# A hand-written order of the opening: the spare maximum on GpSimd earlier, the last copies of x ahead of the transposing DMAs, tiles 12 to 15 split sooner

## The chip, the cores and the metric

One core of a Trainium2 chip runs the kernel. The metric is device time in microseconds (us) of one execution. TensorE (PE) does the matrix products, VectorE (DVE), ScalarE (ACT) and GpSimd (POOL) the elementwise work, SyncE (SP) issues most DMAs, and POOL issues the DMAs that add to memory while they write.

## The reference

A layer norm over 576 features of 2048 rows, and the sum of three terms: x itself, the real part of a two-dimensional DFT of the normed x, and a two-layer MLP of the normed x with 4608 hidden features.

```python
xn = _layernorm(x, axis=-1)
return x + _A_ref(xn, A_dft_seq_re, A_dft_seq_im, A_dft_hid_re, A_dft_hid_im) + _B_ref(xn, B_w1, B_w2)
# _A_ref: a = xn @ re.T, b = xn @ im.T, y = Cr @ a - Ci @ b
# _B_ref: h = max(xn @ w1, 0), y = h @ w2
```

## The kernel before, in words

Every f32 operand is split into two f16 parts, `hi` and `lo`, and a product is made of three f16 products. x is cut into 16 tiles of 128 rows; four tiles are a group (g = 0 to 3). The hidden features are cut into nine blocks. For each block and group the kernel makes the first layer (line 380, eight banks of PSUM in two pools of four), splits the result, and makes the second layer (line 643) as seven products of a Strassen-like scheme over half matrices. Behind the MLP comes the DFT with the same scheme. This text is only about the opening, the first 90 us or so, in which block 0 is worked off for groups 0 to 2.

What happens to a tile t in the opening: `counts` and `moments` take mean and variance on DVE, `stats` does the rest of the layer norm in small steps (one step serves a whole group for tiles 4 to 15), `normal` writes the normed tile in f32, `high_x` its f16 part, `low_x` the difference in two pieces (part 1 has 512 columns, part 0 has 64), `again` copies 128 columns once more. Then the tile is transposed: tiles 0 to 3 by PE, tiles 4 to 15 by a DMA that SP issues (`transposes_dma`, line 336). The four staging places for this lie in one buffer, `dbuf`; tile t uses place t % 4. The split of block 1's w1 (`split_w1`, lines 232 on ACT and 235 on DVE) writes into the same buffer: its first half into the place of tile 12. So that split has to wait until the transposing DMA of tile 12 has read its place. It stands in a list of chores, `todo`, of which each `(work, 0)` takes the next: number 1 issues the two loads of block 1's w1 (line 154), 4 and 5 take maxima of it (line 162), 7 turns them into a scale, 8 and 9 are the split, 10 loads w2, and so on.

`mlp2_mm` n of a group is product n (0 to 6) of the second layer, twelve matmuls; `mlp2_out` n takes it out of PSUM: on ACT for n = 0, 2, 3, 6 (line 658), on DVE for n = 1, 4, 5 (line 662). Products 0, 2, 4, 6 share one place in PSUM, so product 4 may begin only when `mlp2_out` 2 has read the place. After n = 1, 4, 5, 6 POOL issues a DMA (line 665) that adds the result to a buffer in DRAM named `spill`; `copy_x` g fills that buffer with x before (line 879, four DMAs per group). `library` on POOL is a maximum over partitions whose result nobody reads (line 928); it makes POOL load the code for the maxima that come later. `fill` gives PE matmuls on zeros, so that its clock is up when work comes.

The order of all this is a table that is written out in the code. `pinned` calls its entries one after the other and holds each instruction behind the last one on its engine, SP and POOL included, so every engine works off its instructions in the order of the table. After the table a loop over the other blocks and groups follows; its first turn makes products 0 and 1 of group 2 and then the first layer of group 3, which reads the transposed tiles 12 to 15.

Of the kernel before, what the change touches and what calls it, by code (L numbers as in the profile page):

```python
# [32 lines left out]
KM = 4  # L33
REM = D - KM * P
EH = D // 2
NKX = 2 * KM + 1
# [19 lines left out]
def kernel(  # L56
# [848 lines left out]
    V, A, GP = nc.vector, nc.scalar, nc.gpsimd  # L905
# [45 lines left out]
    for f, *a in (  # L951
        (counts, 0),
        (moments, 0),
        (stats, 0),
        (max_w1, 0, 0),
        (stats, 0),
        (fill, 50),
# [3 lines left out]
        (stats, 0),  # L961
        (stats, 0),
        (max_w1, 0, 1),
        (steps_of, wa),
        (counts, 1),
        (high_x, 0),
        (normal, 0, A),
        (steps_of, wa),
        (fill, 4),
        (moments, 1),  # L970
        (stats, 1),
        (counts, 2),
        (stats, 1),
        (transposes, 0, *H),
        (fill, 10),
        (steps_of, wa),
        (steps_of, wa),
        (low_x, 0, 0, V),
        (copies, 0, 0, KM),
        (stats, 1),  # L980
        (steps_of, wa),
        (moments, 2),
        (hi1, 0),
        (stats, 1),
        (low_x, 0, 1, GP),
        (fill, 4),
        (steps_of, wa),
        (fill, 11),
        (transposes, 0, KM, NKX),
        (stats, 1),  # L990
        (stats, 1),
        (max_w1, 0, 2),
        (counts, 3),
        (high_x, 1),
        (moments, 3),
        (normal, 1, A),
        (max_w1, 0, 3),
        (stats, 2),
        (stats, 2),
        (counts, 5),  # L1000
        (stats, 2),
        (fill, 3),
        (low_x, 1, 0, V),
        (hi1, 1),
        (fill, 9),
        (tile_by, 0, (0,), XH[0], True, False),
        (stats, 2),
        (fill, 31),
        (low_x, 1, 1, GP),
        (transposes, 0, *L[1:-1]),  # L1010
        (transposes, 1, *H),
        (fill, 7),
        (transposes, 1, *L[1:-1]),
        (transposes, 1, KM, NKX),
        (copies, 0, KM, NKX + 1),
        (fill, 11),
        (copies, 1, 0, KM),
        (lo1, 0),
        (stats, 2),
        (stats, 2),  # L1020
        (tile_by, 0, (0,), XL, False, False),
        (copies, 1, KM, NKX + 1),
        (steps_of, wb),
        (lo1, 1),
        (steps_of, wb),
        (fill, 9),
        (tile_by, 0, (0,), XH[1], False, True),
        (normal, 2, V),
        (high_x, 2),
        (steps_of, wb),  # L1030
        (steps_of, wb),
        (tile_by, 0, (1,)),
        (low_x, 2, 0, V),
        (steps_of, wb),
        (counts, 4),
        (tile_by, 1, (0, 1), XH[0] + XH[1], True, False),
        (high_x, 3),
        (low_x, 2, 1, GP),
        (normal, 3, V),
        (low_x, 3, 1, GP),  # L1040
        (counts, 6),
        (sum_w2, 0, 0),
        (hi1, 2),
        (transposes, 2, *H),
        (moments, 5),
        (transposes, 2, *L[1:-1]),
        (counts, 7),
        (moments, 6),
        (moments, 4),
        (moments, 7),  # L1050
        (transposes, 2, KM, NKX),
        (copies, 2, 0, NKX + 1),
        (transposes, 3, *H),
        (tile_by, 1, (0, 1), XL, False, True),
        (low_x, 3, 0, GP),
        (lo1, 2),
        (transposes, 3, *L[1:-1]),
        (transposes, 3, KM, NKX),
        (tile_by, 2, (1,)),
        (tile_by, 2, (0,)),  # L1060
        (hi1, 3),
        (stats, 4),
        (stats, 4),
        (tile_by, 0, (2,)),
        (stats, 4),
        (stats, 4),
        (stats, 4),
        (stats, 4),
        (copies, 3, 0, NKX + 1),
        (lo1, 3),  # L1070
        (tile_by, 3, (0,)),
        (high_x, 4),
        (again, 4, GP),
        (tile_by, 2, (2,)),
        (normal, 4, V),
        (counts, 8),
        (normal, 5, A),
        (tile_by, 2, (3,)),
        (counts, 9),
        (counts, 11),  # L1080
        (outputs, 0, 0, "r"),
        (high_x, 5),
        (high_x, 6),
        (moments, 11),
        (tile_by, 1, (2,)),
        (moments, 9),
        (sum_w2, 0, 1),
        (normal, 6, V),
        (counts, 10),
        (tile_by, 3, (1,)),  # L1090
        (normal, 7, A),
        (tile_by, 3, (2,)),
        (steps_of, wb),
        (steps_of, wc),
        (moments, 10),
        (low_x, 4, 0, GP),
        (moments, 8),
        (low_x, 4, 1, GP),
        (stats, 8),
        (counts, 14),  # L1100
        (low_x, 5, 1, GP),
        (outputs, 0, 0, "hA"),
        (tile_by, 0, (3,)),
        (steps_of, wc),
        (stats, 8),
        (high_x, 7),
        (outputs, 0, 0, "hB"),
        (transposes_dma, 4),
        (low_x, 5, 0, GP),
        (low_x, 6, 0, GP),  # L1110
        (again, 6, GP),
        (tile_by, 1, (3,)),
        (stats, 8),
        (stats, 8),
        (again, 7, A),
        (again, 5, GP),
        (stats, 8),
        (stats, 8),
        (low_x, 6, 1, GP),
        (counts, 15),  # L1120
        (normal, 8, V),
        (high_x, 8),
        (normal, 10, A),
        (low_x, 7, 0, GP),
        (steps_of, wc),
        (tile_by, 3, (3,)),
        (transposes_dma, 5),
        (outputs, 0, 0, "s3"),
        (tile_by, 4, (0, 1)),
        (steps_of, wc),  # L1130
        (steps_of, wc),
        (tile_by, 5, (0, 1)),
        (outputs, 0, 1, "r"),
        (steps_of, wc),
        (normal, 9, A),
        (steps_of, wc),
        (low_x, 7, 1, GP),
        (outputs, 0, 0, "lA"),
        (low_x, 8, 0, V),
        (steps_of, wc),  # L1140
        (high_x, 9),
        (again, 8, A),
        (low_x, 8, 1, GP),
        (outputs, 0, 1, "s3"),
        (counts, 13),
        (transposes_dma, 6),
        (outputs, 0, 1, "s2"),
        (steps_of, wc),
        (low_x, 9, 1, GP),
        (high_x, 10),  # L1150
        (outputs, 0, 0, "s2"),
        (transposes_dma, 7),
        (high_x, 11),
        (outputs, 0, 1, "s1"),
        (steps_of, wc),
        (tile_by, 6, (0, 1)),
        (normal, 11, A),
        (tile_by, 7, (0, 1)),
        (outputs, 0, 1, "s4"),
        (outputs, 0, 0, "s4"),  # L1160
        (again, 9, GP),
        (again, 10, A),
        (low_x, 10, 1, GP),
        (outputs, 0, 1, "hA"),
        (steps_of, wc),
        (products, 1, 2),
        (outputs, 0, 1, "hB"),
        (outputs, 0, 0, "lB"),
        (hi2, 0, 0),
        (low_x, 9, 0, V),  # L1170
        (outputs, 0, 0, "s1"),
        (outputs, 0, 1, "lA"),
        (hi2, 1, 0),
        (products, 1, 3),
        (counts, 12),
        (lo2, 0, 0),
        (moments, 15),
        (lo2, 1, 0),
        (outputs, 1, 0, "r"),
        (outputs, 0, 0, "hS"),  # L1180
        (diff2, 0),
        (diff2, 1),
        (outputs, 0, 0, "lS"),
        (outputs, 1, 0, "s3"),
        (low_x, 10, 0, GP),
        (transposes_dma, 8),
        (diff2, 2),
        (low_x, 11, 0, GP),
        (outputs, 1, 0, "hB"),
        (hi2, 0, 1),  # L1190
        (moments, 14),
        (mlp2_mm, 0, 0, 0),
        (outputs, 1, 0, "s2"),
        (outputs, 0, 1, "hS"),
        (outputs, 1, 0, "hA"),
        (diff2, 3),
        (moments, 12),
        (transposes_dma, 9),
        (outputs, 1, 0, "lA"),
        (moments, 13),  # L1200
        (again, 11, GP),
        (outputs, 0, 1, "lB"),
        (hi2, 0, 2),
        (stats, 12),
        (transposes_dma, 10),
        (lo2, 0, 2),
        (low_x, 11, 1, GP),
        (outputs, 1, 0, "lB"),
        (transposes_dma, 11),
        (products, 2, 0),  # L1210
        (products, 2, 1),
        (lo2, 0, 1),
        (copy_x, 0),
        (outputs, 1, 0, "s4"),
        (outputs, 1, 0, "s1"),
        (hi2, 1, 2),
        (mlp2_out, 0, 0, 0),
        (outputs, 0, 1, "lS"),
        (stats, 12),
        (outputs, 1, 1, "r"),  # L1220
        (lo2, 1, 2),
        (copy_x, 1),
        (hi2, 1, 1),
        (outputs, 1, 1, "hB"),
        (outputs, 1, 0, "hS"),
        (mlp2_mm, 0, 0, 1),
        (stats, 12),
        (mlp2_mm, 0, 0, 2),
        (outputs, 2, 0, "r"),
        (mlp2_out, 0, 0, 1),  # L1230
        (library,),
        (lo2, 1, 1),
        (mlp2_out, 0, 0, 2),
        (outputs, 1, 0, "lS"),
        (outputs, 1, 1, "s1"),
        (outputs, 2, 0, "s3"),
        (work, 0),
        (stats, 12),
        (mlp2_mm, 0, 0, 3),
        (stats, 12),  # L1240
        (mlp2_out, 0, 0, 3),
        (mlp2_mm, 0, 0, 4),
        (stats, 12),
        (normal, 14, A),
        (mlp2_out, 0, 0, 4),
        (outputs, 1, 1, "hA"),
        (outputs, 1, 1, "s3"),
        (mlp2_mm, 0, 0, 5),
        (work, 0),
        (outputs, 1, 1, "s2"),  # L1250
        (mlp2_mm, 0, 0, 6),
        (high_x, 15),
        (outputs, 1, 1, "s4"),
        (outputs, 1, 1, "lA"),
        (outputs, 2, 0, "s2"),
        (high_x, 13),
        (products, 2, 2),
        (high_x, 14),
        (work, 0),
        (mlp2_out, 0, 0, 5),  # L1260
        (outputs, 2, 0, "s1"),
        (normal, 15, A),
        (outputs, 1, 1, "lB"),
# [435 lines left out]
    A = {}  # L1699
# [241 lines left out]
```

## Time and profile before

| | us |
|---|---|
| three runs: lowest, median, highest | 1219.42, 1223.31, 1224.68 |
| the profiled execution, its own time | 1222.13 |
| its span, from the first to the last instruction | 1220.4 |
| PE busy in the span | 1210.1 |
| PE busy from the first layer of group 3 (83.70) to the end | 1132.85 of 1136.7 |

Times below are microseconds from the start of the span. A row of a timeline merges neighbouring instructions of one kind: start, duration, engine, line, operation, out <- in, count, and in brackets the idle time ahead of it and what ended it.

### The profile page before, as it was taken

The page shows a single profiled execution, that of the slowest core. Times are in us where ns is not written, and L with a number is a line of the kernel's source. Part 1 is how long each engine was busy: PE and PEld are TensorE (multiplying, and loading weights), DVE is VectorE, ACT ScalarE, POOL GpSimd, SP SyncE. Part 2 cuts the span into 40 slices and gives each one's busy share as a digit, 9 for nine tenths or more (in the row PEclk, how much of TensorE's full clock was granted, in tenths as well). Part 3 has the DMA queues.
Part 4 walks back from the last instruction along what each step waited for, and adds up shares of the span by engine and source line. Part 5 has one row for each costly group of instructions (what it writes and reads, how often), then busy time and mean ns, then how long its engine had stood idle before and what let it go on. Part 6 is the DMA issues. An engine that isn't in the chain of part 4 may idle for free.

```text
span 1220.4 us, 24658 instructions
## 1 busy us (share of the span) xinstructions
PE 1210.1 (99%) x10233; PEld 958.5 (79%) x10233; DVE 1007.9 (83%) x1642; ACT 724.4 (59%) x1082; POOL 161.0 (13%) x199
## 2 busy tenths in 40 slices
PE   9989999999999999999999999999999999999998
PEld 8656567888888888888888888877777777777776
DVE  9988999887797788788877977678898978787875
ACT  7755565876676766757767766555644433433332
POOL 3231211111121211111121211100000000000000
PEclk9999999999999999999999999999999999999999
DMA  7895554867667675667576676520165254534320
GB/s 259 197 189 127 99 96 107 168 135 164 155 128 169 131 185 128 136 156 156 127 172 159 120 166 155 98 31 1 62 215 169 72 185 138 177 109 146 101 89 20
DMA packets 84064, 164.66 MB, mean 135 GB/s; under 512 B 22640, under 2 KB 43632, under 8 KB 83952
## 3 DMA queue, kind: packets, MB, share of 16 engines
q1 hardware_dynamic: 61168, 120.61, 31.1%
q0 software_dynamic: 22784, 42.48, 24.7%
q8 instruction: 80, 1.31, 0.4%
q14 instruction: 32, 0.26, 0.1%
HBM read 110.76 MB, written 53.08 MB: 134 GB/s over the span
## 4 chain that ended last, share of the span: by engine, by line
PE 94%; DMA 2%; DVE 2%; ACT 1%; issue 0%; SPq 0%; DVEq 0%; ACTq 0%
PE p L643 29%; PE p L1841 27%; PE bank L548 22%; PE p L380 7%; PE U L1630 4%; PE W L1630 2%; PE bank L567 1%; PE V L1630 1%; DMA arena<-in_x_dram 1%; DMA arena<-in_cim_dram 1%; DMA arena<-arena 1%; DVE arena L235 1%; DMA arena<-in_cre_dram 0%; ACT arena L232 0%; PE U L1646 0%
## 5 line engine op out<-in xcount | busy, mean ns | idle before, releaser
L643 PE MATMUL p<-arena 128*128 128x288 f16 x3024 | 398.6, 286 | 1.8 <-DVE arena L662 1.8
L643 PEld LDWEIGHTS <-arena 128*128 128x128 f16 x3024 | 295.9, 98 | 77.3 <-issue 2.2
L1841 PE MATMUL p<-arena 128*128 128x288 f16 x2688 | 329.4, 286 | 0.0
L1841 PEld LDWEIGHTS <-arena 128*128 128x128 f16 x2688 | 263.0, 98 | 66.3
L548 PE MATMUL bank<-arena 128*128 128x256 f16 x2580 | 304.8, 273 | 0.0
L548 PEld LDWEIGHTS <-arena 128*128 128x128 f16 x2580 | 250.2, 98 | 37.4 <-issue 5.9
L232 ACT ACTIVATE arena<-arena,sc_c 128x1024 f16<-128x1024 f32 x112 | 128.5, 1149 | 189.8 <-PE p L1841 137.8
L665 POOL DMA_DIRECT2D spill<-arena x144 | 128.7, 912 | 547.2 <-DVE arena L662 454.0
L235 DVE SCALAR_TENSOR_TENSOR arena<-arena,sc_c 128x1024 f16<-128x1024 f32 x112 | 143.3, 1280 | 29.4 <-ACT arena L232 26.4
L658 ACT ACTIVATE arena<-p,c_ub 128x576 f32<-128x576 f32 x144 | 105.9, 735 | 45.5 <-PE p L643 40.7
L235 DVE SCALAR_TENSOR_TENSOR arena<-arena,c_sw 128x640 f16<-128x640 f32 (+2 forms) x118 | 96.5, 848 | 32.5 <-ACT arena L232 30.6
L662 DVE SCALAR_TENSOR_TENSOR arena<-p,c_ub,arena 128x576 f32<-128x576 f32 x108 | 87.8, 813 | 22.2 <-PE p L643 19.6
L380 PE MATMUL p<-arena 128*128 128x128 f16 (+1 forms) x680 | 100.0, 303 | 3.1 <-issue 2.8
L576 DVE TENSOR_TENSOR arena<-bank,arena 128x512 f32<-128x512 f32 x84 | 57.7, 687 | 54.2 <-PE bank L548 53.2
L573 ACT ACTIVATE arena<-bank 128x512 f32<-128x512 f32 x112 | 66.5, 594 | 52.0 <-PE bank L548 51.9
L232 ACT ACTIVATE arena<-arena,c_sw 128x640 f16<-128x640 f32 (+2 forms) x118 | 89.3, 793 | 9.4 <-issue 4.5
L1630 PEld LDWEIGHTS <-arena 128*128 128x128 f16 x738 | 71.6, 98 | 19.7 <-issue 1.9
L380 PEld LDWEIGHTS <-arena 128*128 128x128 f16 x680 | 52.4, 98 | 43.3 <-issue 7.4
L579 ACT ACTIVATE arena<-arena 128x512 f16<-128x512 f32 x84 | 52.9, 630 | 52.5 <-DVE arena L576 51.6
L1849 DVE SCALAR_TENSOR_TENSOR arena<-p,us_c,arena 128x288 f32<-128x288 f32 x112 | 57.4, 513 | 27.0 <-PE p L1841 26.6
L1491 ACT ACTIVATE arena<-arena 128x1024 f32<-128x1024 f32 x64 | 67.0, 1047 | 7.6 <-DMA arena<-in_cim_dram 6.0
L589 DVE TENSOR_TENSOR arena<-arena 128x1024 f16<-128x1024 f32 x56 | 68.1, 1217 | 0.3 <-ACT arena L585 0.3
(134 smaller groups left out, 1050.4 us busy)
## 6 DMA issues: line engine op xcount, KB each, us to landing
spill<-arena POOLq DMA_DIRECT2D x144, 288.0 KB, 5.1
arena<-in_cre_dram SPq DMA_DIRECT2D x64, 512.0 KB, 4.6
arena<-in_cim_dram SPq DMA_DIRECT2D x64, 512.0 KB, 4.8
arena<-in_w_dram SPq DMA_DIRECT2D x17, 640.0 KB, 5.8
arena<-in_w_dram SPq DMA_DIRECT2D x18, 576.0 KB, 4.0
arena<-spill SPq DMA_DIRECT2D x40, 144.0 KB, 2.2
arena<-in_x_dram SPq DMA_DIRECT2D x16, 288.0 KB, 7.0
spill<-in_x_dram SPq DMA_DIRECT2D x16, 288.0 KB, 6.9
```

The costliest lines, as they stand in the source:

```text
L232: nc.scalar.activation(hi, src, AF.Copy, scale=s)
L235: nc.vector.scalar_tensor_tensor(lo, src, s, hi, ALU.mult, ALU.subtract)
L380: order["m1"] = nc.tensor.matmul(ps[:, cols], w1s[b, i // 2][:, hl, i % 2 * KT + k], xT[g][:, kx, cols], start=(start and n == 0), stop=(s ...
L548: nc.tensor.matmul(ps[:, i], l, r, start=first and i == m == 0, stop=m == len(todo) - 1, skip_group_check=not first or i > 0,)
L589: order["lo"] = nc.vector.tensor_tensor(lo, stage[:, 1 + 2 * i :][:, :2], hi, ALU.subtract).ins
L643: order["pe"] = nc.tensor.matmul(ps[:, c], h[:, x, qa, c * P : (c + 1) * P], w[:, y, qb], start=first and i == 0 and j == 0, stop=i == NQ ...
L658: freed(nc.scalar.activation(o, ps, AF.Copy, scale=us[b]))
L662: add = nc.vector.scalar_tensor_tensor(o, ps, us[b], o, ALU.mult, ALU.add)
L665: nc.gpsimd.dma_start(spill[g, row, col], o, accum_op=ALU.add)
L1491: nc.scalar.activation(f, f, AF.Abs, scale=2.0**-10, accum_out=sums_c[:, n, q : q + 1])
L1630: nc.tensor.matmul(ps, l, r, start=first and m == 0, stop=m == len(todo) - 1, skip_group_check=not first,)
L1841: nc.tensor.matmul(ps, w[:, a, k], r[:, c, RQ[rq]], start=first and k == 0 and j == 0, stop=k == HK - 1 and j == 2, skip_group_check=not f ...
```

## The change

The table keeps its 383 entries, and nearly all stand at another place. Thirteen operations on x change their engine (`normal`, `low_x` and `again` of tiles 2, 5, 6, 8 and 11 to 14). No computation is added or left out. Of the diff, which is 690 lines long, these are its beginning, the place of `library`, and the stretch in which tiles 12 to 15, the copies of x for groups 2 and 3 and the chores stand:

```diff
     for f, *a in (
+        (fill, 50),
         (counts, 0),
         (moments, 0),
-        (stats, 0),
-        (max_w1, 0, 0),
-        (stats, 0),
-        (fill, 50),
         (fill, 25),
         (stats, 0),
         (stats, 0),
         (stats, 0),
+        (max_w1, 0, 0),
         (stats, 0),
         (max_w1, 0, 1),
+        (stats, 0),
+        (stats, 0),
         (steps_of, wa),
...
+        (lo2, 0, 2),
+        (copy_x, 0),
+        (lo2, 1, 2),
+        (library,),
         (stats, 12),
...
-        (library,),
...
+        (low_x, 12, 1, V),
+        (mlp2_mm, 0, 1, 1),
+        (low_x, 15, 0, V),
+        (outputs, 1, 1, "hS"),
+        (copy_x, 2),
+        (copy_x, 3),
...
+        (outputs, 1, 1, "lS"),
+        (transposes_dma, 12),
+        (low_x, 13, 1, V),
+        (transposes_dma, 13),
+        (mlp2_mm, 0, 1, 2),
+        (again, 15, A),
+        (mlp2_out, 0, 1, 1),
+        (outputs, 2, 0, "hA"),
+        (low_x, 15, 1, V),
+        (outputs, 2, 0, "s1"),
+        (work, 0),
+        (work, 0),
+        (outputs, 2, 1, "hB"),
         (outputs, 2, 0, "s2"),
...
+        (mlp2_out, 0, 1, 2),
+        (outputs, 2, 1, "s2"),
+        (mlp2_mm, 0, 1, 4),
...
-        (low_x, 14, 1, V),
-        (transposes_dma, 12),
-        (outputs, 2, 1, "s3"),
...
-        (copy_x, 2),
-        (work, 0),
```

The engines' own order at three places. SP, behind the first eight transposing DMAs and the copies for groups 0 and 1; before:

```order
L154 DMA arena_63<-in_w1_dram 128x1280 x2
L336 DMA_TRANSPOSE arena_63<-arena_63 128x10x128 x4
L879 DMA spill2_00_78<-in_x_dram 256x1x288
L879 DMA spill2_01_79<-in_x_dram 256x1x288
L879 DMA spill2_10_80<-in_x_dram 256x1x288
```

and now:

```order
L154 DMA arena_63<-in_w1_dram 128x1280 x2
L879 DMA spill2_00_78<-in_x_dram 256x1x288
L879 DMA spill2_01_79<-in_x_dram 256x1x288
L879 DMA spill2_10_80<-in_x_dram 256x1x288
L879 DMA spill2_11_81<-in_x_dram 256x1x288
L879 DMA spill3_00_82<-in_x_dram 256x1x288
L879 DMA spill3_01_83<-in_x_dram 256x1x288
L879 DMA spill3_10_84<-in_x_dram 256x1x288
L879 DMA spill3_11_85<-in_x_dram 256x1x288
L336 DMA_TRANSPOSE arena_63<-arena_63 128x10x128 x4
```

The eight copies for groups 2 and 3 (`spill2`, `spill3`) stand ahead of the transposing DMAs of tiles 12 to 15; the rest of SP's queue is as it was.

POOL, from the last subtraction of the opening on (`none` is the maximum that nobody reads, `top` a maximum of w1 of block 1, `spill0_00` what product 1 of group 0 adds); before:

```order
L322 TENSOR_TENSOR arena_63<-arena_63 128x512
L665 DMA spill0_00_70<-arena_63 256x1x288
L928 ISA
L928 ISA none_1100<-eps_105 128x1
L665 DMA spill0_11_73<-arena_63 256x1x288
L665 DMA spill0_01_71<-arena_63 256x1x288
L665 DMA spill0_10_72<-arena_63 256x1x288
L665 DMA spill1_00_74<-arena_63 256x1x288
L168 ISA top_1301<-c_mw1_1249 128x1
```

and now:

```order
L322 TENSOR_TENSOR arena_63<-arena_63 128x64
L928 ISA
L928 ISA none_1081<-eps_105 128x1
L665 DMA spill0_00_70<-arena_63 256x1x288
L665 DMA spill0_11_73<-arena_63 256x1x288
L665 DMA spill0_01_71<-arena_63 256x1x288
L168 ISA top_1183<-c_mw1_1176 128x1
L665 DMA spill0_10_72<-arena_63 256x1x288
L665 DMA spill1_00_74<-arena_63 256x1x288
```

The code load and its maximum stand ahead of the first adding DMA instead of behind it, and the maximum of w1 stands one adding DMA sooner than the last of group 0.

ACT, around product 2 of group 1 (`p2_0_1_0` is the place of products 0, 2, 4, 6 of group 1, `p2_0_1_3` that of 3 and 5; line 232 with `c_sw1` is the split of w1, line 434 the relu of a first-layer bank); before:

```order
L658 ACTIVATE arena_63<-p2_0_1_0_1201,c_ub_860 128x2x288
L432 ACTIVATE arena_63<-p1_0_2_2_1173 128x256
L658 ACTIVATE arena_63<-p2_0_1_3_1277,c_ub_860 128x2x288
L232 ACTIVATE arena_63<-arena_63,c_sw1_1250 128x640
L440 ACTIVATE arena_63<-arena_63 128x4x256
L434 ACTIVATE arena_63<-p1_0_2_3_1231 128x2x256
L232 ACTIVATE arena_63<-arena_63,c_sw1_1250 128x640
```

and now:

```order
L232 ACTIVATE arena_63<-arena_63,c_sw1_1177 128x640 x2
L434 ACTIVATE arena_63<-p1_0_2_3_1251 128x2x256
L434 ACTIVATE arena_63<-p1_0_2_1_1042 128x2x256
L658 ACTIVATE arena_63<-p2_0_1_0_1209,c_ub_896 128x2x288
L658 ACTIVATE arena_63<-p2_0_1_3_1303,c_ub_896 128x2x288
```

Both halves of the split of w1 stood behind the taking out of products 2 and 3; now they stand ahead of it. On DVE the two subtractions of the split move in the same way ahead of the taking out of products 4 and 5 of group 1.

## Rows read from the trace of the kernel before

**Rows 1.** Windows: length, PE busy (matmuls), granted clock, DMA share, GB/s

```profile
83.70:1220.40 1136.70, 1132.85 (x9400) 1.00 0.54 130
```

**Rows 2.** Timeline of PE, the opening

```profile
20.66 7.98 PE L380 MATMUL p<-arena 128*128 128x128 f16 x140
...
68.76 7.51 PE L643 MATMUL p<-arena 128*128 128x288 f16 x60
77.84 3.10 PE L643 MATMUL p<-arena 128*128 128x288 f16 x24 [1.57 <-DVE arena L662]
83.70 4.41 PE L380 MATMUL p<-arena 128*128 128x512 f16 x13 [2.76 <-issue]
...
88.58 2.98 PE L380 MATMUL p<-arena 128*128 128x512 f16 x13
```

**Rows 3.** Windows of PE, columns as in rows 1

```profile
84.70:85.70 1.00, 1.00 (x4) 0.50 1.11 311
```

**Rows 4.** Timeline of SP

```profile
49.99 4.62 SPq L154 DMA_DIRECT2D arena<-in_w_dram  x2
68.37 11.65 SPq L336 DMA_TRANSPOSE arena<-arena  x4
80.07 6.23 SPq L879 DMA_DIRECT2D spill<-in_x_dram  x8
```

**Rows 5.** DMA issues of 68.3 to 69: KB each, median us from issue to landing

```profile
arena<-arena SPq DMA_TRANSPOSE x1, 7.7
```

**Rows 6.** The same for 53 to 54, and for 78 to 79

```profile
spill<-arena POOLq DMA_DIRECT2D x1, 288.0 KB, 6.4
...
arena<-arena SPq DMA_TRANSPOSE x1, 6.9
```

**Rows 7.** Timeline of POOL

```profile
53.84 1.40 POOL L665 DMA_DIRECT2D spill<-arena  x1 [15.07 <-DMA arena<-in_w_dram]
62.82 1.30 POOL L928 PARTITION_ALL_REDUCE none<-eps  x1 [7.58 <-issue]
64.01 4.63 POOL L665 DMA_DIRECT2D spill<-arena  x4
```

**Rows 8.** Timelines of ACT and DVE where the split of w1 waits

```profile
76.10 0.83 ACT L232 ACTIVATE arena<-arena,c_sw 128x640 f16<-128x640 f32 x1 [1.31 <-DMA arena<-arena]
...
76.18 0.88 DVE L235 SCALAR_TENSOR_TENSOR arena<-arena,c_sw 128x640 f16<-128x640 f32 x1 [1.90 <-DMA arena<-arena]
76.98 0.81 DVE L662 SCALAR_TENSOR_TENSOR arena<-p,c_ub,arena 128x576 f32<-128x576 f32 x1
```

**Rows 9.** Timeline of ACT, single instructions

```profile
74.21 0.58 ACT L434 ACTIVATE arena<-p 128x512 f16<-128x512 f32 x1
...
77.78 0.72 ACT L658 ACTIVATE arena<-p,c_ub 128x576 f32<-128x576 f32 x1
```

**Rows 10.** Windows with DMA rates: length, POOL busy, clock, DMA share, GB/s

```profile
55.50:57.50 2.00, 0.00 (x0) 1.00 0.80 218
...
59.50:64.50 5.00, 1.68 (x2) 1.00 0.04 8
66.00:71.00 5.00, 2.64 (x3) 1.00 1.14 152
...
75.00:77.00 2.00, 0.66 (x1) 1.00 1.45 239
...
85.50:90.50 5.00, 1.10 (x1) 0.88 1.09 364
```

**Rows 11.** Timelines of DVE and ACT, the start

```profile
15.42 0.16 DVE L299 SCALAR_TENSOR_TENSOR sh<-mv,r 128x2 f32<-128x2 f32 x1
...
16.30 0.27 DVE L210 TENSOR_REDUCE top<-pm 1x1 bf16<-1x128 f32 x1
...
17.52 1.16 ACT L738 ACTIVATE arena<-arena 128x1152 f16<-128x1152 f32 x1
...
19.39 1.22 ACT L350 ACTIVATE arena<-pt 128x1280 f16<-128x1280 f16 x1
```

More of the change, by code (lines that the diff above doesn't have):

```diff
@@ L983 @@
+        (low_x, 0, 1, GP),
         (hi1, 0),
         (stats, 1),
-        (low_x, 0, 1, GP),
-        (fill, 4),
+        (high_x, 1),
         (steps_of, wa),
-        (fill, 11),
[L989 to L997, printed above, removed]
+        (max_w1, 0, 2),
+        (normal, 1, A),
+        (counts, 3),
+        (moments, 2),
+        (moments, 3),
@@ L998 @@
+        (stats, 2),
+        (fill, 7),
+        (counts, 4),
+        (hi1, 1),
+        (transposes, 1, *H),
+        (tile_by, 0, (0,), XH[0], True, False),
+        (transposes, 0, *L[1:-1]),
+        (stats, 2),
+        (low_x, 1, 1, GP),
+        (transposes, 0, KM, NKX),
+        (copies, 0, KM, NKX + 1),
+        (max_w1, 0, 3),
+        (fill, 11),
         (stats, 2),
+        (low_x, 1, 0, V),
         (stats, 2),
-        (counts, 5),
+        (transposes, 1, *L[1:-1]),
+        (copies, 1, 0, KM),
@@ L1001 @@
+        (lo1, 1),
         (stats, 2),
[L1002 to L1029, printed above, removed]
         (steps_of, wb),
         (steps_of, wb),
+        (transposes, 1, KM, NKX),
+        (stats, 2),
+        (fill, 9),
+        (lo1, 0),
+        (normal, 2, V),
+        (copies, 1, KM, NKX + 1),
@@ L1032 @@
+        (normal, 3, V),
         (tile_by, 0, (1,)),
-        (low_x, 2, 0, V),
         (steps_of, wb),
-        (counts, 4),
+        (steps_of, wb),
+        (high_x, 2),
+        (low_x, 2, 1, GP),
+        (low_x, 2, 0, GP),
+        (steps_of, wb),
+        (counts, 7),
+        (high_x, 3),
+        (counts, 6),
+        (moments, 7),
+        (low_x, 3, 0, GP),
+        (counts, 5),
+        (moments, 4),
+        (tile_by, 0, (0,), XL, False, False),
+        (transposes, 2, *H),
+        (tile_by, 0, (0,), XH[1], False, True),
@@ L1036 @@
+        (sum_w2, 0, 0),
         (tile_by, 1, (0, 1), XH[0] + XH[1], True, False),
-        (high_x, 3),
-        (low_x, 2, 1, GP),
-        (normal, 3, V),
+        (moments, 6),
         (low_x, 3, 1, GP),
-        (counts, 6),
-        (sum_w2, 0, 0),
+        (moments, 5),
+        (transposes, 3, *H),
+        (transposes, 2, *L[1:-1]),
         (hi1, 2),
[L1044 to L1049, printed above, removed]
@@ L1063 @@
         (stats, 4),
-        (tile_by, 0, (2,)),
[L1065 to L1074, printed above, removed]
+        (sum_w2, 0, 1),
+        (stats, 4),
+        (lo1, 3),
+        (steps_of, wc),
+        (high_x, 4),
+        (tile_by, 2, (0,)),
+        (tile_by, 2, (2,)),
+        (again, 4, GP),
+        (copies, 3, 0, NKX + 1),
@@ L1085 @@
         (tile_by, 1, (2,)),
+        (high_x, 7),
+        (again, 7, A),
         (moments, 9),
[L1087 to L1091, printed above, removed]
-        (tile_by, 3, (2,)),
-        (steps_of, wb),
-        (steps_of, wc),
[L1095 to L1102, printed above, removed]
@@ L1147 @@
[L1147 to L1153, printed above, removed]
+        (outputs, 0, 0, "hA"),
+        (low_x, 6, 0, V),
+        (low_x, 5, 1, GP),
+        (again, 5, GP),
+        (normal, 7, A),
+        (stats, 8),
+        (moments, 15),
+        (stats, 8),
+        (transposes_dma, 5),
+        (counts, 12),
+        (outputs, 0, 1, "r"),
+        (low_x, 6, 1, GP),
@@ new lines @@
+        (outputs, 1, 1, "hA"),
+        (mlp2_mm, 0, 0, 2),
+        (high_x, 14),
+        (outputs, 1, 1, "s3"),
+        (mlp2_mm, 0, 0, 3),
+        (again, 14, A),
+        (mlp2_out, 0, 0, 2),
+        (outputs, 1, 1, "s2"),
+        (copy_x, 1),
+        (mlp2_out, 0, 0, 3),
+        (mlp2_mm, 0, 0, 4),
+        (work, 0),
+        (normal, 12, A),
+        (work, 0),
+        (work, 0),
+        (normal, 14, V),
+        (outputs, 1, 1, "lB"),
+        (outputs, 2, 0, "r"),
+        (outputs, 1, 1, "s4"),
@@ L1313 @@
[L1313 to L1319 removed]
+        (high_x, 15),
+        (low_x, 14, 0, V),
+        (products, 2, 2),
+        (mlp2_out, 0, 0, 6),
+        (mlp2_mm, 0, 1, 0),
+        (work, 0),
+        (low_x, 12, 1, V),
[4 more added lines that the diff above has]
+        (copy_x, 3),
```

381 lines of the change are left out of this document (176 added, 205 removed).

## The prediction

> **What bounds the kernel now.** I read first how busy PE is behind the opening. From the first layer of group 3 (83.70) to the end it is busy for 1132.85 of 1136.7 us [rows 1], so whatever brings that layer forward or back is worth its full length, and nothing behind it can be gained by this change. Next, the timeline of PE in the opening [rows 2]: from 20.66 on it has two gaps worth a name, 1.57 us ahead of 77.84 and 2.76 ahead of 83.70, both in the first turn of the loop. A third loss hides behind the second gap: PE goes on at its lower clock, 1.2 GHz [rows 3], and the 13 matmuls at 83.70 take 4.41 us where the same 13 at 88.58 take 2.98 [rows 2]: 1.43 lost. So 1.57 + 2.76 + 1.43 = 5.8 us are to be had at most, 0.5% of the time.
>
> Then, what ended these gaps. The long one: the first layer of group 3 reads the transposed tiles 12 to 15. SP issues their four DMAs from 68.37 on and takes 11.65 us for it [rows 4]; the last lands 6.9 us after its issue [rows 6], so one issued at 76.8 lands at 83.7, where PE starts. The short one: the DMA of tile 12 lands at 68.37 + 7.7 = 76.07 [rows 4, 5]. The split of w1 writes into its place, so ACT and DVE start that at 76.10 and 76.18, and the taking out of product 5 stands behind it on DVE at 76.98; PE waits for that [rows 2, 8].
>
> Why do the transposing DMAs take so long? POOL shows it: behind its first adding DMA (53.84) it loads code for 7.58 us and makes the unread maximum (1.30), then issues four adding DMAs in a row from 64.01 [rows 7]. The DMA engines, idle from 59.5 to 64.5 (share 0.04), are full from 66 on with these four alone, at 152 GB/s [rows 10]. One moves 0.295 MB, so it takes 1.94 us; four take 7.8. Tile 12's DMA comes behind them.
>
> **The change, part by part.** I call L the time at which the DMA of tile 12 lands.
>
> The unread maximum moves ahead of the first adding DMA, into the 15.07 us in which POOL has nothing to do [rows 7]. It needs 7.58 + 1.30 = 8.9 us, so it costs nothing; were that cover gone, the adding DMAs would come late by the rest, as now. The adding DMAs of products 4, 5 and 6 of group 0 then go as their products come out, about 59 to 63, and not in a bunch from 64 to 68.6.
>
> The eight copies of x move ahead of the transposing DMAs. SP is idle from 54.6 to 68.37 and needs 6.23 us for the issues [rows 4], so SP has room. But the copies move 2.36 MB, at the 364 GB/s of the stretch in which they ran before (with loads of w2) 6.5 us [rows 10], and now in the same stretch as the adding DMAs.
>
> Tiles 12 to 15 are split sooner. Tile 12's last subtraction stood on DVE behind the taking out of product 1 of group 1; now it follows product 5 of group 0 and two maxima, by my count some 4 us sooner, so its DMA can be issued at about 64 instead of 68.37. That counts only if the DMA engines are free then.
>
> They are not. The queue, worked out from landings: the first adding DMA landed at 53.84 + 6.4 = 60.2, behind the second load of w1 [rows 6, 7]; with a shift of 0.5 us (the start, below) that is 60.7. Behind it now stand the copies, 6.5 us, the adding DMAs of products 4, 5, 6, 3 x 1.94 = 5.8, and tile 12's DMA itself, 0.328 MB at the 239 GB/s at which it moved before [rows 10], 1.4. So L = 60.7 + 6.5 + 5.8 + 1.4 = 74.4, little sooner than 76.07. The low end is that the adding DMAs don't hold it at all: 68.6. The high end is that the copies run at the 218 GB/s at which a load and an adding DMA shared the engines [rows 10]: 10.8 instead of 6.5, L = 78.7. I take 74.4, since before, too, tile 12's DMA landed only when the adding DMAs issued ahead of it, 7.8 us of work, were through [rows 5, 7].
>
> The Trainium skill ("DMA: Bandwidth & Descriptors", Queues, rings and completion order) says that each DMA engine takes the queues it has work for in turns, packet by packet. By that rule tile 12's DMA would wait only for the copies in its own queue and share with what is left of the others; as an estimate it would come 1.5 us sooner, L = 72.9, and the sum below would end at 1221.1. The 7.7 us behind four adding DMAs [rows 5] don't look like turns.
>
> Now the order on ACT decides. Both halves of the split of w1 stand ahead of the taking out of product 2 of group 1. The second half waits for L; then come itself (0.83), two relus (0.58 each) and the taking out (0.72) [rows 8, 9], less 0.2 of overlap: product 4 can start at L + 2.5. PE would be there at 68.76 + 2 x 1.47 + 0.5 = 72.2 (60 matmuls in 7.51 are five products, 1.47 each from start to start) [rows 2]. So PE stands still from 72.2 to 76.9, 4.7 us, longer than the gap of 2.76 behind which the clock was low [rows 2, 3], and I count the same 1.4 us for it. On DVE, behind L, come two subtractions (1.7), four small operations (1.4), two maxima (1.6) and one more (0.3), then the taking out of product 4 at about L + 5; the product itself ends at L + 2.5 + 2.9, so nothing more waits. Then products 4, 5, 6 of group 1 and 0, 1 of group 2: 5 x 1.47 = 7.35. The first layer of group 3 starts at L + 2.5 + 1.4 + 7.35 = L + 11.3, now at full clock, and its 13 matmuls end 2.98 later, L + 14.2 = 88.6, against 88.1 before. Tile 15's DMA landed 83.7 - 76.07 = 7.6 us behind tile 12's before; again so, that is 82.0, ahead of L + 11.3 = 85.7: no wait. **The two old gaps go, a new one of the same size comes at product 4: +0.5 us.**
>
> The start. Two steps of tile 0's norm now stand behind the second maximum of w1, 0.3 us later; a reduce of 0.27 (line 210) moves ahead of tile 2's last step, and small steps add 0.2. So that step goes from 15.42 to about 16.3 [rows 11]. Behind it on ACT stand two `high_x`, `sum_w2` (1.16), `hi1` and the copy of tile 2 (1.22), about 4.8 in sum: 21.2. Before, that copy ended at 20.61 and the run of 140 matmuls began at 20.66 [rows 2, 11]. So PE is about 0.6 late there and 0.5 at the second layer. Bounds: 0, if the steps overlap better, and 1.5, if ACT and DVE each lose one operation more. It enters only through the 60.7, since PE waits at product 4 in any case. The thirteen operations that change their engine lie beside a PE that has no gap from 20.66 to the second layer, and cost nothing; with that cover gone, the dearest (a `normal`) costs 0.8.
>
> **Sum.** The profiled execution took 1222.13, 1.2 less than the median of the runs shown, 1223.31. 1222.13 + 0.5 = 1222.6. In general, time = 1222.13 + (L - 73.9). At its best, with L under 69.7 where PE no longer waits, it is 1222.13 - 5.8 + 0.5 = 1216.8.
>
> **The rivals.** (a) The forecast, L from 73 to 77: 1221 to 1225. Chance 0.50. (b) The adding DMAs hold the transposing ones less than I think, or the copies end sooner: L from 68.6 to 72.5, time 1216.8 to 1220.7. For it speaks that copies and transposes are in one queue and the adding DMAs in another; against it rows 5. Chance 0.25. (c) Slower: copies and adding DMAs, which ran apart before, slow each other. If the copies come down to the 152 GB/s that the adding DMAs reach alone [rows 10], they take 15.5 us, L = 83.4 and the time is 1231.6. It decides from L = 80 on, where the copies get under about 195 GB/s. The 218 of a shared stretch speaks against it. Chance 0.08. (d) The start or the middle is later than 0.6: product 0 of group 0 needs the last split of w2's first part, which by my adding up is ready only 0.7 us ahead of PE, and a wait there adds to the 60.7 as well: 1223.5 to 1227. Chance 0.17.
>
> **How the numbers follow.** About 0.5%, 6.1 us, is what a measurement of this kernel tells from no change. (a) and most of (b) and (d) lie within it. Faster by more than that needs the low end of (b), all 5.8 us and a little more: 0.05. Slower needs (c), or (d) at its worst: 0.08. Within: 0.87. For the range I leave out the last part of (b) below 1217.5, (c), and the end of (d): 1217.5 to 1227.
>
> **What would show it.** Right: POOL makes the unread maximum between 40 and 50; the adding DMAs of group 0 are spread from 54 to 64; the copies are issued from 55 to 62; the wait of 2.76 at the first layer of group 3 is gone; PE waits for ACT (line 658) at product 4 of group 1, and the granted clock is low behind it; tile 12's DMA lands at 73 to 77. Wrong: no such wait and the first layer of group 3 at 80 or sooner (b); a wait over 8 us (c); gaps of PE between 21 and 51 (d).

## The result

The changed kernel takes 1227.6 us in the median of ten runs (1225.42 to 1229.90), the kernel before, run beside it on the same chip, 1222.63 (1218.27 to 1227.64). The ratio is 1.0041, with a 95% interval of 1.0022 to 1.0059: slower by 5 us, and 0.6 us above the range that was forecast. The profiled execution took 1229.81 and its span is 1228.0, so it lies at the slow end of its runs. A second set on another chip (the first experiment) gave 1.0070, from 1.0051 to 1.0089. The change makes the kernel slower by 0.4 to 0.7%.

PE in the opening, the changed kernel's timeline (start, duration, line, shape, count, idle time ahead and what ended it); it answers to [rows 2]:

```profile
21.30 3.29 PE L380 MATMUL p<-arena 128*128 128x128 f16 x56
...
46.04 6.20 PE L380 MATMUL p<-arena 128*128 128x512 f16 x28 [0.61 <-DMA arena<-arena]
52.08 8.98 PE L643 MATMUL p<-arena 128*128 128x288 f16 x72
...
83.00 10.37 PE L643 MATMUL p<-arena 128*128 128x288 f16 x60 [10.02 <-ACT arena L658]
93.21 2.97 PE L380 MATMUL p<-arena 128*128 128x512 f16 x13
```

Both old gaps (1.57 and 2.76) are gone. In their place stands one of 10.02 at product 4 of group 1, behind it 60 matmuls take 10.37 instead of 7.51, and at the second layer of group 0 (52.08) PE is 1.1 later than before, where that row reads:

```profile
50.96 8.98 PE L643 MATMUL p<-arena 128*128 128x288 f16 x72
```

The first 13 matmuls of the first layer of group 3 end at 93.21 + 2.97 = 96.18 instead of 83.70 + 4.41 = 88.11 [rows 2], 8.1 us late; the spans of the two profiled executions differ by 7.6, so the loss is made in the opening.

What was waited for, ACT and DVE in the same stretch, beside [rows 8]:

```profile
66.69 0.83 ACT L232 ACTIVATE arena<-arena,c_sw 128x640 f16<-128x640 f32 x1
79.59 0.83 ACT L232 ACTIVATE arena<-arena,c_sw 128x640 f16<-128x640 f32 x1 [12.07 <-DMA arena<-arena]
80.32 0.58 ACT L434 ACTIVATE arena<-p 128x512 f16<-128x512 f32 x1
81.72 0.60 ACT L434 ACTIVATE arena<-p 128x512 f16<-128x512 f32 x1 [0.82 <-DVE arena L438]
82.21 1.37 ACT L658 ACTIVATE arena<-p,c_ub 128x576 f32<-128x576 f32 x2
```

ACT comes to the second half of the split of w1 at 67.5 and stands there for 12.07 us until tile 12's DMA has landed; two relus and the taking out of product 2 (82.21) queue behind it, and PE starts 0.8 later. This is the wait that the prediction described, at its place and in its order. Its length is what was wrong.

Its origin, SP's timeline, beside [rows 4]:

```profile
55.82 10.00 SPq L879 DMA_DIRECT2D spill<-in_x_dram  x8
65.93 15.19 SPq L336 DMA_TRANSPOSE arena<-arena  x4
```

and POOL's, beside [rows 7]:

```profile
47.74 0.39 POOL L928 PARTITION_ALL_REDUCE none<-eps  x1 [5.89 <-DMA spill<-in_x_dram]
54.96 1.40 POOL L665 DMA_DIRECT2D spill<-arena  x1 [6.83 <-DMA spill<-in_x_dram]
...
63.31 1.11 POOL L665 DMA_DIRECT2D spill<-arena  x1
68.37 1.08 POOL L665 DMA_DIRECT2D spill<-arena  x1 [3.96 <-DVE arena L662]
```

The unread maximum is out of the way at 48, and the adding DMAs of group 0 go at 54.96, 59.43, 60.74 and 63.31, as forecast. The DMA issue of tile 12 (count, us from issue to landing), beside [rows 5]:

```profile
arena<-arena SPq DMA_TRANSPOSE x1, 13.6
```

And four windows of the changed kernel (length, PE busy with its matmuls, granted clock, DMA share, GB/s):

```profile
64.00:72.00 8.00, 8.00 (x57) 1.00 1.16 254
72.50:76.50 4.00, 0.48 (x4) 0.84 0.97 59
76.50:79.50 3.00, 0.00 (x0) 0.50 1.22 202
84.00:88.00 4.00, 4.00 (x19) 0.50 0.14 56
```

Tile 12's DMA, issued at 65.9, lands at 65.9 + 13.6 = 79.5. Until 72 the DMA engines move copies and added results together at 254 GB/s. Then, for 4 us, all engines are called busy and move 59 GB/s; I call this the standstill. The trace of packets shows what stands: 16 packets of 256 bytes, the size of the transposing DMA's packets, begin between 72.3 and 72.8 and all end at 76.6. PE's clock is at its lower level (1.2 GHz, 0.50) in the later part of the gap and still from 84 to 88, in the work behind it.

### The profile page after: what moved, and what is told of

It reads as the page before. It is cut to its first block, busy times and chain, and to the rows that moved or that the text cites. A ratio compares the mean times of both kernels' runs of the same rounds, so it can differ in the third digit from the quotient of the medians.

```text
span 1228.0 us, 24652 instructions
## 1 busy us (share of the span) xinstructions
PE 1212.1 (99%) x10233; PEld 960.6 (78%) x10233; DVE 1009.6 (82%) x1643; ACT 724.0 (59%) x1081; POOL 160.5 (13%) x199
## 4 chain that ended last, share of the span: by engine, by line
PE 95%; DMA 2%; DVE 1%; POOL 0%; issue 0%; ACT 0%; SPq 0%; POOLq 0%; DVEq 0%
PE p L643 30%; PE p L1841 27%; PE bank L548 23%; PE p L380 6%; PE U L1630 4%; PE W L1630 2%; DMA arena<-arena 1%; PE bank L567 1%; PE V L1630 1%; POOL arena L322 0%; DMA arena<-in_x_dram 0%; DVE st L271 0%; DVE arena L235 0%; PE U L1646 0%; PE p L405 0%
```

## The experiments

Each ratio is to runs of the kernel before on the same chip, with its 95% interval. The theory T is that of the prediction's own chain: copies of x ahead of the transposing DMAs make tile 12's DMA late, the early split of w1 hands that on to PE.

**The changed kernel again** (no edit).

> The changed kernel once more, for a second look at its opening and a second set of times. Theory T (the copies of x, now ahead of the transposing DMAs, make the DMA of tile 12 late; the split of w1 waits for it on ACT and DVE, and product 4 of group 1 waits behind the split; PE then runs some us at its lower clock): about 1227.5, and a wait of PE for line 658 of 6 to 10 us. Rival S (the 4 us in which packets of the transposing DMA stood still on all 16 engines were an accident of the one profiled execution): that wait is 5 to 6 us here and no such standstill is seen. Rival R (the later start and the new wait of 0.6 us at tile 11 cost most): the wait for line 658 under 5 us at the same 1227.5.

1229.94 us, 1.0070 (1.0051 to 1.0089). PE's timeline at product 4:

```profile
84.21 9.14 PE L643 MATMUL p<-arena 128*128 128x288 f16 x60 [11.65 <-ACT arena L658]
```

and a window ahead of it:

```profile
72.00:76.00 4.00, 0.56 (x5) 1.00 1.21 91
```

The wait, 11.65 us, is longer than the 6 to 10 that T expected, the time 2.4 us over its 1227.5, and the standstill is there again (91 GB/s for 4 us). Neither is an accident of one execution; rivals S and R fall.

**Copies and split, each taken back, and both.** The three edits to the changed table:

```diff
-        (copy_x, 2),
-        (copy_x, 3),
...
         (transposes_dma, 15),
+        (copy_x, 2),
+        (copy_x, 3),
```

```diff
         (mlp2_out, 0, 1, 4),
+        (work, 0),
...
         (mlp2_out, 0, 1, 5),
+        (work, 0),
+        (work, 0),
```

(in the second, five `(work, 0)` ahead of them go, so that chores 8 to 10 stand where these are; the last two of the five come at the end of the table), and the two together.

> The changed kernel with the eight copies of x for groups 2 and 3 back behind the transposing DMAs of tiles 12 to 15; all else as changed. T: without the copies ahead of it the DMA of tile 12 lands at 60.7 + 5.8 + 1.4 = 67.9, at the latest at 70; PE comes to product 4 of group 1 at about 73 and does not wait; the clock stays up: 1217 to 1219. Rival S (the transposing DMA stands still by itself, whatever runs beside it): it lands at 72 to 74, PE waits 2 to 4 us, 1220 to 1223. Rival R (the start and tile 11 cost the time): 1226 to 1228.

> The changed kernel with the split of the next block's w1 back behind the taking out of products 4 and 5 of group 1; the copies stay ahead of the transposing DMAs. T: tile 12's DMA is as late as in the changed kernel (77 to 80), but product 4 of group 1 starts at about 73 without a wait for line 658; PE comes to the first layer of group 3 at about 80.5 and waits there for tile 15, which lands at about 83, with some 1.4 us at the low clock behind it: 1221 to 1224, about the time of the kernel before. Rival (the lateness of the transposing DMAs costs the same wherever it is waited for): 1226 to 1228, with a wait of 7 us or more at the first layer of group 3. Rival R (start and tile 11): 1226 to 1228 with waits no longer than before.

> The changed kernel with both taken back: the copies of x behind the transposing DMAs, and the split of w1 behind the taking out of products 4 and 5 of group 1. T: tile 12's DMA lands by 70, nothing waits for it, and PE has no gap behind the second layer of group 0: 1217 to 1219, the same as with the copies alone taken back, since the early split costs nothing once the DMA is in time. Rival (the early split puts work of ACT and DVE ahead of PE's in any case): 2 us or more below the kernel with the copies alone taken back. Rival R (start and tile 11): 1226 to 1228.

| | split early | split back |
|---|---|---|
| copies ahead | 1229.94, 1.0070 (the changed kernel again) | 1223.05, 1.0020 (1.0007 to 1.0033) |
| copies back | 1217.49, 0.9976 (0.9966 to 0.9986) | 1218.99, 0.9987 (0.9976 to 0.9998) |

All four ran on one chip, where the kernel before took 1219.95. The copies alone are worth 12.5 us with the early split and 4.1 without; the early split costs 6.9 when tile 12 is late, and nothing when it is in time (the 1.5 in its favour there comes from a chore that my edit shifted, below). With the copies back, tile 12's DMA needs 5.2 us and lands at 65.3 + 5.2 = 70.5, ACT's split starts there (ACT's timeline, copies back, split early),

```profile
70.55 0.83 ACT L232 ACTIVATE arena<-arena,c_sw 128x640 f16<-128x640 f32 x1 [2.72 <-DMA arena<-arena]
```

and PE waits 0.66 us, at full clock (PE's timeline of the same kernel):

```profile
73.96 7.51 PE L643 MATMUL p<-arena 128*128 128x288 f16 x60 [0.66 <-ACT arena L658]
81.30 2.97 PE L380 MATMUL p<-arena 128*128 128x512 f16 x13
```

With only the split back, ACT again waits for the DMA, until 78.25, but behind the taking out of products 2 and 3 (ACT's timeline, copies ahead, split back):

```profile
78.25 0.83 ACT L232 ACTIVATE arena<-arena,c_sw 128x640 f16<-128x640 f32 x1 [3.30 <-DMA arena<-arena]
```

Product 4 starts without a wait: the 60 matmuls from 70.36 on, products 2 to 6 of group 1, are one run (PE's timeline of the same kernel):

```profile
70.36 7.51 PE L643 MATMUL p<-arena 128*128 128x288 f16 x60
80.66 2.24 PE L643 MATMUL p<-arena 128*128 128x288 f16 x17 [2.79 <-DVE arena L662]
84.63 1.03 PE L643 MATMUL p<-arena 128*128 128x288 f16 x7 [1.73 <-DVE half L171]
```

T's times hold in all three, its details not everywhere. With the copies back tile 12 landed at 70.5, where T had 70 at the latest. In the kernel with the split back the wait came at product 0 of group 2 and not at the first layer of group 3, and a further 1.73 comes from chores that my edit shifted, not from the copies: DVE takes two maxima of w1 first, and its step on the next maximum (line 171) ends that wait. The kernel with both taken back, which was to have no gap, has 0.23 and the same 1.73.

**The unread maximum alone, the copies alone, and these two, on the order before.** The edits, on the table of before:

```diff
         (transposes_dma, 11),
+        (library,),
...
-        (library,),
```

```diff
         (work, 0),
+        (copy_x, 2),
+        (copy_x, 3),
...
-        (copy_x, 2),
...
-        (copy_x, 3),
```

(the `(work, 0)` is the one that issues the loads of w1).

> The kernel before with one edit: the unread maximum (with the loading of its code) directly behind tile 11, as the change has it; the copies of x, the split of w1 and the start stay as before. T: the adding DMAs of group 0 are spread from 54 to 64, tile 12's DMA, issued at 68.4 as before, meets nearly free DMA engines and lands about 5 us later, at 73 to 74 (with the copies taken back it took 5.2 us); the gap of 1.57 goes and the gap at the first layer of group 3 shrinks below 2: 2 to 4.5 us under the kernel before of the same chip. Rival (the landing is set by SP's slow issues and the transposing DMA itself): within 1 us of the kernel before, tile 12 at 75.5 or later.

> The kernel before with one edit: the eight copies of x directly behind the loads of w1, ahead of the transposing DMAs; the unread maximum, the split of w1 and the start as before. T (the copies harm because they share the DMA engines with the adding DMAs just when the transposing DMA wants them): here they run from 55 to about 64, in which the adding DMAs don't, so tile 12 lands at 76 to 77.5 and the time is within 2 us of the kernel before. Rival Q (copies in the same queue ahead of a transposing DMA harm wherever they run): tile 12 at 79 or later, 3 us or more over the kernel before.

> The order before with two edits: the unread maximum directly behind tile 11, and the eight copies of x directly behind the loads of w1; the split of w1, tiles 12 to 15 and the start as before. With the first alone 1215.8 was measured, with the second alone 1221.95, with neither 1218.84. If the two add up: 1215.8 + 3.1 = 1218.9. T (the copies and the spread adding DMAs, running together, slow each other, and the transposing DMAs behind them): tile 12 lands at 76 or later and the time is 1221 to 1226. Rival (the copies are through before 68.4, when tile 12's DMA is issued): tile 12 at 73 to 74, 1216 to 1218.

| | copies as before | copies ahead |
|---|---|---|
| maximum as before | 1 | 1.0023 (1.0008 to 1.0038), 1221.95 us |
| maximum behind tile 11 | 0.9964 (0.9952 to 0.9977), 1215.80 us | 0.9983 (0.9970 to 0.9996), 1218.28 us |

The maximum alone is the best kernel of this study (the kernel with both taken back, which still has the new start and the shifted chores, comes to 0.9987): PE has no gap over 0.4 us from its first long run (20.25) through the opening. Its PE, SP and POOL timelines:

```profile
68.48 10.45 PE L643 MATMUL p<-arena 128*128 128x288 f16 x84
79.07 2.97 PE L380 MATMUL p<-arena 128*128 128x512 f16 x13
```

```profile
68.09 7.28 SPq L336 DMA_TRANSPOSE arena<-arena  x4
```

```profile
60.59 2.19 POOL L665 DMA_DIRECT2D spill<-arena  x2 [1.52 <-DVE arena L662]
```

Tile 12's DMA finds nearly free engines and lands 4.5 us behind its issue instead of 7.7 [rows 5], at 72.6; SP needs 7.28 us for the four instead of 11.65 [rows 4]. The copies alone were expected to change nothing much, and cost 0.23%: the unread maximum came late, while the copies ran beside the load of its code (POOL's and SP's timelines, copies alone),

```profile
65.26 0.38 POOL L928 PARTITION_ALL_REDUCE none<-eps  x1 [10.61 <-DMA spill<-in_x_dram]
```

```profile
67.77 15.41 SPq L336 DMA_TRANSPOSE arena<-arena  x4
```

10.61 us of waiting instead of 7.58 [rows 7], the four adding DMAs went 1.5 us later, and tile 12 landed at 78.4. So T's numbers missed, and rival Q's nearly held (79, and 3 us over the kernel before: 3.1), by a cause that neither had named. This profile is of an execution of 1226.38 us, near the slow end of its twelve (1219.89 to 1226.71), so the usual landing is likely sooner. Together the two edits about add up (0.36% gained, 0.23% lost, 0.17% left, the last on another chip); my forecast that they do worse than add up fell. Tile 12 was late all the same (68.3 + 8.1 = 76.4, with a standstill from 72 to 75), but with the split in its old place PE waited for only 1.95 us of it (a window and PE's timeline, both edits):

```profile
72.00:75.00 3.00, 3.00 (x27) 1.00 1.37 65
```

```profile
78.17 4.77 PE L643 MATMUL p<-arena 128*128 128x288 f16 x24 [1.95 <-DVE arena L662]
```

**The changed kernel with the maximum back, and with the copies sooner.**

```diff
-        (library,),
...
         (mlp2_out, 0, 0, 1),
+        (library,),
```

```diff
         (copy_x, 1),
+        (copy_x, 2),
+        (copy_x, 3),
...
-        (copy_x, 2),
-        (copy_x, 3),
```

> The changed kernel with the unread maximum back behind product 1 of group 0; copies ahead of the transposing DMAs and early split as changed. T: the copies run without adding DMAs beside them and are through by about 64, then come the four adding DMAs in a row, 7.8 us; tile 12, issued at about 65.5, lands at 74 to 77, and PE waits 4 to 7 us for line 658: 1222 to 1226, some 3 us under the changed kernel. Rival (the place of the unread maximum is worth what the change meant by it): 1228 or more, above the changed kernel. Rival Q (copies harm wherever they run): tile 12 at 79 or later, 1228.

> The changed kernel with the eight copies of x directly behind those of groups 0 and 1, ahead of the loads of w1; still ahead of the transposing DMAs, but issued some 8 us sooner. T: the copies are through by about 62, before the transposing DMA of tile 12 is issued at 65.9, and two adding DMAs are left beside it: tile 12 at 71 to 73, a wait for line 658 of 0 to 2 us, 1218 to 1221, if the loads of w1, now behind the copies, don't come late for DVE's maxima. Rival Q: tile 12 at 78 or later and 1226 to 1230. Rival W: the loads of w1 come late, DVE waits for them and PE for DVE: 1224 or more, with a wait on loads of w1 in the waits.

1225.08 us (1.0046, 1.0032 to 1.0060) and 1223.13 (1.0020, 1.0006 to 1.0035), beside 1.0041 and 1.0070 for the changed kernel. In the first the copies and adding DMAs run one after the other, and tile 12 lands at 75.6, inside T's range, though its DMA was issued only at 69.48 instead of 65.5; PE's wait for line 658 is 3.40 us, less than expected, but 1.50 more stand ahead of it, since DVE waits 5.26 for POOL's next maximum. The time is in T's range, but not the 3 us under the changed kernel that T had: its ratio lies between that kernel's two. In the second rival W had the mechanism, and its time (1224 or more) missed by 0.9: the loads of w1, now behind the copies, come late, and DVE's maxima with them, and tile 12, issued at 70.93, lands at 75.2 (DVE's timeline, copies sooner):

```profile
66.48 1.54 DVE L162 TENSOR_REDUCE c_mf<-arena 128x1 f32<-128x640 f32 x2 [5.72 <-DMA arena<-in_w_dram]
```

Neither tells much about the copies, because each edit moved another wait.

**Half the copies, and the copies behind tile 12.**

```diff
         (copy_x, 2),
-        (copy_x, 3),
...
         (transposes_dma, 15),
+        (copy_x, 3),
```

```diff
-        (copy_x, 2),
-        (copy_x, 3),
...
         (transposes_dma, 12),
+        (copy_x, 2),
+        (copy_x, 3),
```

> The changed kernel with half of the dose: the four copies of x for group 2 stay ahead of the transposing DMAs, the four for group 3 go back behind them. T: tile 12 lands half way between 70.5 (no copies ahead) and 79.5 to 80.8 (eight), at 74 to 76; PE waits 2.5 to 5 us for line 658: 1220 to 1225. Rival (the standstill of the transposing DMA comes wherever any copy is ahead): tile 12 at 78 or later, 1226 to 1230. Rival (four copies are through in time): tile 12 at 71 to 72, at most 1218.5.

> The changed kernel with the eight copies of x directly behind the transposing DMA of tile 12, ahead of those of tiles 13 to 15. T: tile 12 lands at 70 to 72, so product 4 of group 1 waits under 1.5 us; tiles 13 to 15, now behind the copies, land at 83 to 88, and PE, which comes to the first layer of group 3 at about 81, waits there 2 to 7 us: 1219.5 to 1226, the wait at another place than in the changed kernel. Rival (only tile 12 matters): 1217 to 1219, no wait at the first layer of group 3.

1218.36 us (0.9979, 0.9966 to 0.9991) and 1226.61 (1.0047, 1.0031 to 1.0064).

ACT's and PE's timelines with half the copies:

```profile
70.36 0.83 ACT L232 ACTIVATE arena<-arena,c_sw 128x640 f16<-128x640 f32 x1 [3.51 <-DMA arena<-arena]
```

```profile
73.77 7.51 PE L643 MATMUL p<-arena 128*128 128x288 f16 x60 [1.45 <-ACT arena L658]
```

Four copies cost nothing that can be measured: tile 12 lands at 70.3, as with none ahead. So it is not the number of bytes ahead in the queue that counts, as T had it; what goes with a late landing is that copies are still running when the transposing DMA is issued. Four are through by then, as the queue rows (packets, MB, share of 16 engines) of 64.2 to 65.5 show: q0 is the adding DMAs', q1 SP's queue, and tile 12's DMA is issued at 64.34.

```profile
q0 software_dynamic: 228, 0.25, 116.3%
q1 hardware_dynamic: 12, 0.01, 3.4%
```

Eight are not (the queue rows of the changed kernel's second profile, below). From issue to landing tile 12's DMA took 8.1 to 15.8 us in the four profiles in which copies ran at its issue (the changed kernel twice, the split back, both edits on the order before) and 4.3 to 6.1 in seven others. The last two, the kernel before (7.7) and the copies alone (10.6, with the copies through), had four adding DMAs issued in a row just ahead of it: copies are not the only company that delays it.

With the copies behind tile 12 the wait for line 658 shrinks to 0.31 and comes back, 6.59 us long, where tiles 13 to 15 are read, with the low clock behind it (13 matmuls in 5.13 instead of 2.97; PE's timeline):

```profile
72.47 7.51 PE L643 MATMUL p<-arena 128*128 128x288 f16 x60 [0.31 <-ACT arena L658]
86.57 5.13 PE L380 MATMUL p<-arena 128*128 128x512 f16 x13 [6.59 <-issue]
```

Tile 12 itself landed at 69.1. That second wait is right; the time, 1226.6, is 0.6 over the range expected.

## Why the prediction was wrong

The mechanism was forecast: the two old gaps go, and a new wait comes at product 4 behind the early split. The step that failed is a term of the sum, the last in the queue of the DMA engines, "tile 12's DMA itself, 0.328 MB at the 239 GB/s at which it moved before [rows 10], 1.4".

- **The queue ahead of tile 12** came out right. It was to be through at 60.7 + 6.5 + 5.8 = 73.0; the full stretch at 254 GB/s ends at 72.5, and tile 12's first packets of 256 bytes move at 71.8. Partly this is luck: the copies and the adding DMAs did not follow one another at their old rates but ran together, SP needed 10.00 us and not 6.23 for the issues of the copies, and a fifth adding DMA was in the queue that the sum had left out.
- **Tile 12's own data** took not 1.4 us but 7 (72.5 to 79.5). Of that, 4.0 are the standstill, in which 351 packets moved where the 8 us ahead of it moved 1998. The rest went in company: packets of tile 13's DMA and of the adding DMA of product 1 of group 1, issued at 68.37, the fifth one, moved beside tile 12's. Without a standstill of that length, in the kernel with the split back, tile 12 still landed only at 78.3. So L was 79.5 instead of 74.4. The bounds had given room to the copies (L up to 78.7) and none to this term. It was too small without any copies, too: from its first 256-byte packet to its landing tile 12 took 2.4 us with the maximum alone, 3.2 with the copies back, 4.5 in the kernel before. The 239 GB/s were the rate of the best stretch there, 75 to 77, when the adding DMAs were nearly through; just ahead of it that kernel has a short standstill of its own, below.
- **From L to product 4** it was 3.5 us and not 2.5: the second relu waited 0.82 for DVE, whose two subtractions I had put behind L without asking who waits for what follows them.
- **The low clock** cost 10.37 - 7.51 = 2.9 us instead of 1.4. The loss behind the old gap of 2.76 was taken for it. The length of the gap alone does not price it either: in the second profile of the changed kernel the same 60 matmuls lost 9.14 - 7.51 = 1.6 behind a gap of 11.65.
- **The start** was right: in the four profiles with the old start the long run begins at 19.98 to 20.66, mean 20.4, in the nine with the new one at 20.63 to 21.71, mean 21.2, so 0.8 later for 0.6 forecast. Missing was the wait of 0.61 for tile 11 at 46.04, 0.17 to 0.63 in all nine and in none of the four.
- **The sum**: time = 1222.13 + (L - 73.9) with the L that was measured gives 1227.7. The profiled execution, in which L was measured, took 1229.8; the relu (1.0) and the clock (1.5) cover the 2.1 between. The forecast 0.5, with the 5.1 by which L was off and these two, makes 8.1, the lateness at the first layer of group 3. That the median, 1227.6, agrees with the sum is partly chance.

A window of the kernel before, ahead of the 75 to 77 of [rows 10], with the columns of the windows above:

```profile
73.50:74.50 1.00, 1.00 (x10) 1.00 1.13 81
```

Of the rivals, (c) came closest: a wait of over 8 us was its sign, and from L = 80 on it was to decide. But its mechanism, copies that are through late, is not what happened. Copies and adding DMAs did slow each other: from 66 to 69 the second profile of the changed kernel has 332 adding packets and 0.36 MB of copies, 120 GB/s instead of 364 [rows 10], and the kernel before has 382 adding packets in the same stretch. The queue rows of the changed kernel, then of the one before:

```profile
q0 software_dynamic: 332, 0.35, 71.5%
q1 hardware_dynamic: 331, 0.36, 43.1%
```

```profile
q0 software_dynamic: 382, 0.42, 115.0%
```

Yet together they moved 254 GB/s and were through in time. (d) ended at 1227, as near to the time, but PE had no gap of its kind: 0.61 was the longest between 21 and 51. (b) was wrong on this kernel and right on the one with the copies back: L = 70.5, 1217.5 us.

The 332 and 331 packets of these rows look like turns, and I had set turns aside on the strength of one row [rows 5]. The Trainium skill ("DMA: Bandwidth & Descriptors", Queues, rings and completion order) says that each DMA engine takes the queues it has work for in turns, packet by packet; the trace agrees. But the time that I had worked out by that rule, L = 72.9, is further from 79.5 than the 74.4 of the sum: the rule says who goes next, not what a mixture costs.

What stays open: why the engines stand still. The three profiles that show 3 to 4 us of it (the changed kernel twice, the two edits on the order before) start a transposing DMA while copies and adding DMAs run; the kernel with the split back does so too and has 76 GB/s for only 1.5 us (74 to 75.5). Shorter ones come without copies: besides that of the kernel before, 58 GB/s for 1 us with the copies back (71.5 to 72.5), 83 from 76 to 78 in the kernel with the copies sooner, and, with the copies long through, in the kernel with the copies alone:

```profile
72.50:75.00 2.50, 2.50 (x22) 1.00 1.54 92
```

So running copies go with the long ones, but the standstill does not need them, and no run shows what sets its length.

## What to carry to other kernels

A transfer that something waits for must be priced in the company it will have, not at the rate of a stretch in which it ran alone; list every DMA that will be in flight when it starts, those issued later on other queues too. A change of several parts should be tried part by part: here one line, the unread maximum ahead of the first adding DMA, gave 0.36%, and the other parts took that and more away. Moving a wait ahead of other work in an engine's order cost nothing here as long as it was met, and nearly its full length with a low clock on top when it wasn't, so it belongs behind what PE needs next.

## What the runs showed of the hardware

- In three of four profiles in which a transposing DMA was issued among copies and adding DMAs, all DMA engines nearly stopped for 3 to 4 us (59, 91 and 65 GB/s); in the first of them 16 of its packets end together. The cause is open. SP's issues were slow in such company, with a standstill or without: four transposing DMAs took 15.19 us to issue in the changed kernel, 7.59 of them tile 12's alone, 14.60 in the one with the split back, and 7.28 when the engines were nearly free.
- Alone, tile 12's kind of DMA moved quickly; mixed with adding DMAs it did not. In the kernel with half of the copies SP's queue moved 1362 packets in 1.5 us with next to no adding packets, in the one with the split back 865 in 3.5 us beside 235 adding ones. The queue rows of the two, 69.5 to 71 and 74.5 to 78:

```profile
q1 hardware_dynamic: 1362, 0.34, 109.8%
q0 software_dynamic: 38, 0.04, 23.4%
```

```profile
q1 hardware_dynamic: 865, 0.21, 70.7%
q0 software_dynamic: 235, 0.25, 60.4%
```

- POOL waits longer for the code of its unread maximum beside eight copies: 10.61 us with the copies alone and 9.66 in the changed kernel with the maximum back, against 7.58 in the kernel before and 5.87 to 6.79 in the ten profiles that have it ahead of the first adding DMA. That the DMA engines are what the two share was not tested.
- A longer gap is not always followed by the low clock. With the split back, gaps of 2.79 and 1.73 us left the granted clock at 1.00 throughout; in the changed kernel with the maximum back it stood at 0.50 from 74 to 76, behind gaps of only 1.50 and 0.30, and 12 matmuls took 2.85 us instead of 1.63. A window of that kernel:

```profile
74.00:76.00 2.00, 1.66 (x7) 0.50 1.18 244
```
